# Sliding-window attention into a two-layer MLP: other runs for the query loads, casts and fills at other steps, and a finer token grouping

## The chip, the cores and the metric

The kernel runs on one core of one Trainium2 chip. The metric is the device time of one execution in microseconds, as the median of several runs. The core's engines (TensorE, VectorE, ScalarE, GpSimd, and SyncE, here SP) each work through their own instructions in order and wait for each other on semaphores. Nearly all DMAs are issued from SP's queue.

## The reference

```python
# q, k, v: (8, 8, 576, 64) float32;  w_in (512, 2048), w_out (2048, 512)
scores = matmul(q, k.transpose(0, 1, 3, 2)) / sqrt(64)
mask = abs(pos[:, None] - pos[None, :]) <= 32
attn = softmax(where(mask, scores, -1e9))
x = matmul(attn, v).transpose(0, 2, 1, 3).reshape(8 * 576, 512)
h = x @ w_in
return maximum(0.01 * h, h) @ w_out          # (4608, 512)
```

Each token attends to the 65 tokens around it, eight heads are put side by side to 512 features, and an MLP with a leaky ReLU follows.

## The kernel before

**Two schemes.** Heads are worked in pairs (`NPAIR` = 4 pairs, index `p`). Batches 0 and 1 (`BY_DMA` = 2) are transposed on TensorE. Batches 2 to 7 are loaded as float32 (`load_qk`, L68), cast to bf16 on GpSimd (`cast_qk`, L258, into `qb` and `kb`) and transposed by a DMA (`transpose_dma`, L281): the keys straight into `kz`, the queries into a tile `kT`, from which VectorE copies the two heads to separate places in `qz` (`place_queries`, L293). Values are loaded by `load_v_pairs` (L103, five DMAs for two pairs) into one buffer `vbuf`, and `cast_vw` (L274) casts them into `vw`, where columns of ones beside them give the softmax's sums in the same matmul. The other half of `qz` must be zero (`clear_q`), the padding of `kz` too, and the ones must be set (`ready`, L226); all of this is filled once per buffer set (`sets`, two of them, used by even and odd batches), over space that batches 0 and 1 used before.

**Steps.** One step of the new scheme is one head pair and 256 tokens, taken as four blocks of 64: `score_blocks` (L348) multiplies each block's queries with 128 keys, ScalarE takes the exponential, GpSimd multiplies by `band`, and two steps later `product_blocks` (L364) multiplies by the values and ones, ScalarE moves the sums, and VectorE takes the reciprocal and scales into `xT`. `step` (L558) does step i's product and step i + 2's score, then the queued work: `qk_due` says at which step a pair is cast and transposed, `v_due` when its values are cast. `base(b)` is the first step with tokens of batch b; batch 3's is 24. Right after the cast, `load_qk` and `load_v_pairs` refill the float32 tiles for the next batch. `chore` lets one more fill be issued per call.

**Groups.** The MLP runs over groups of tokens: four of 288 (batches 0 and 1), then two of 256, five of 512 and one of 384. For each group come 16 hidden tiles (`h_tile`: four matmuls, then one eviction by ScalarE with the leaky ReLU, `h_out`), later the output tiles of 128 tokens (`o_tile`: 16 matmuls, one eviction, one store). Hidden and output tiles share four PSUM accumulators (`mmps`).

**Order.** The order is written out by hand up to group 1. From there a small planner adds up the matmul time of hidden and output tiles into a clock and spreads the steps over it (`due`), so that a group's tokens are ready 5 us of that clock before its hidden tiles begin; `spend` runs the steps that are due. SP's queue follows the same program order: loads, transposes and stores are issued one behind the other, each also waiting until the eighth DMA before it has landed.

Of the kernel before, what the change touches and what calls it, by code (L numbers as in the profile page):

```python
# [10 lines left out]
BF16 = mybir.dt.bfloat16  # L11
AF = mybir.ActivationFunctionType
# [4 lines left out]
def kernel(  # L17
# [6 lines left out]
    moe_w_out: bass.AP,  # L24
    out: bass.AP,
):

# [4 lines left out]
    nc = tc.nc  # L32

    B, H, S, D = q.shape
    W = 32
# [4 lines left out]
    NPAIR = H // 2  # L40
    NB = S // 64
# [7 lines left out]
    const = ctx.enter_context(tc.tile_pool(name="const", bufs=1))  # L49
# [13 lines left out]
    qf, kf, vf = {}, {}, {}  # L63
    RUN = S // 96

    BY_DMA = 2

    def load_qk(b, p, behind=None):  # L68

        for into, src, name in ((qf, q, "qf"), (kf, k, "kf")):
            t = fload.tile([96, 2, RUN * D], FP32, name=f"{name}{p}")
            if behind is not None:
                behind.memset(t[0:1, 0, 0:1], 0.0)
                behind = None
            heads = src[b, 2 * p:2 * p + 2]
            if b < BY_DMA:
                nc.sync.dma_start(out=t, in_=heads.rearrange("a (p c) d -> p a (c d)", c=RUN))
            else:  # L80
                nc.sync.dma_start(
                    out=t.rearrange("p a (c d) -> p a c d", d=D),
                    in_=heads.rearrange("a (c p) d -> p a c d", p=96),
                )
            into[b, p] = t
# [17 lines left out]
    def load_v_pairs(b, p):  # L103

        r = slice(2 * p, 2 * p + 4)
        heads = v[b, r]
        for n in range(5):
            rows = slice(W if n == 0 else 0, 128 - W if n == 4 else 128)
            at = 128 * n - W
            nc.sync.dma_start(  # L110
                out=vtile[rows, r, n],
                in_=heads[:, at + rows.start:at + rows.stop].rearrange("a p d -> p a d"),
            )
# [29 lines left out]
    KPAD = S + 2 * W  # L143
    N_Q, N_K, N_V, N_BD = NPAIR * 2 * S, NPAIR * KPAD, NPAIR * NB * 3 * D, NPAIR * NB * 128
    N_SET = N_Q + N_K + N_V
    sets = [const.tile([128, N_SET], BF16, name=f"set{i}") for i in range(2)]
    qT, kbd, vbd, qz, kz, vw = [], [], [], [], [], []
    for t in sets:
        qT.append(t[:, 0:NPAIR * S].rearrange("p (n s) -> p n s", n=NPAIR))
        kbd.append(t[:, N_SET - 2 * N_BD:N_SET - N_BD].rearrange(  # L150
            "p (n m j) -> p n m j", n=NPAIR, j=128))
        vbd.append(t[:, N_SET - N_BD:].rearrange("p (n m j) -> p n m j", n=NPAIR, j=128))
        qz.append(t[:, 0:N_Q].rearrange("p (n a s) -> p n a s", n=NPAIR, a=2))
        kz.append(t[:, N_Q:N_Q + N_K].rearrange("p (n s) -> p n s", n=NPAIR))
        vw.append(t[:, N_Q + N_K:].rearrange("p (n m c d) -> p n m c d", n=NPAIR, c=3, d=D))
# [42 lines left out]
        lo = (16, 0)[hf]  # L198
        nc.gpsimd.tensor_copy(out=mask[hf][:, 1, :, lo:lo + 128], in_=win_f[:, :, 0:128])

    band = const.tile([128, 8, D], BF16)

    def make_band():

        nc.gpsimd.memset(band, 1.0)
        yield
        nc.gpsimd.affine_select(
            out=band, in_=band, compare_op=ALU.is_ge, fill=0.0,
            base=0, channel_multiplier=1, pattern=[[0, 8], [-1, D]],
        )  # L210
        yield
        nc.gpsimd.affine_select(
            out=band, in_=band, compare_op=ALU.is_ge, fill=0.0,
            base=2 * W, channel_multiplier=-1, pattern=[[0, 8], [1, D]],
        )
        yield

    band_parts = make_band()

    def clear_q(i):  # L220
        for p in range(NPAIR):
            for a in range(2):
                nc.vector.memset(qz[i][64 * (1 - a):64 * (1 - a) + 64, p, a], 0.0)
                yield

    def ready(i):  # L226

        nc.vector.memset(kz[i][:, :, 0:W], 0.0)
        nc.vector.memset(kz[i][:, :, KPAD - W:], 0.0)
        yield  # L230
        for p in range(NPAIR):
            nc.vector.memset(vw[i][:, p, :, 1], 1.0)
            yield
        nc.vector.memset(vw[i][0:W, :, 0, 1], 0.0)
        nc.vector.memset(vw[i][128 - W:128, :, NB - 1, 1], 0.0)
        yield

    NPROB = 6
# [12 lines left out]
    OLD = 8 * BY_DMA  # L251
# [22 lines left out]
    def cast_vw(b, p):  # L274

        to, src = vw[b % 2][:, p], vf[b, p].rearrange("p a s d -> p s a d")
        nc.gpsimd.tensor_copy(out=to[:, 0::2, 0:3:2], in_=src)  # L277
        nc.gpsimd.tensor_copy(out=to[0:64, 1::2, 0:3:2], in_=src[64:128, 0:4])  # L278
        nc.gpsimd.tensor_copy(out=to[64:128, 1::2, 0:3:2], in_=src[0:64, 1:5])  # L279

    def transpose_dma(b, p):  # L281
        t = kt.tile([128, S], BF16, name="kT")
        for to, src in ((t, qb), (kz[b % 2][:, p, W:W + S], kb)):
            nc.sync.dma_start_transpose(
                out=to.rearrange("p (c i) -> p c i", c=RUN),
                in_=src[:, p].rearrange("p c a d -> p (c a d)"),
            )
# [60 lines left out]
    def score_blocks(i):  # L348
        p, bs = i % NPAIR, blocks_of(i)
        n = 2 * 64 * len(bs)  # L350
        lo = 512 * (i % 2)
        sc = ps[:, lo:lo + n].rearrange("p (a w i) -> p a w i", a=2, i=64)
        for w, (b, m) in enumerate(bs):
            nc.tensor.matmul(  # L354
                sc[:, :, w], kz[b % 2][:, p, 64 * m:64 * m + 128],
                qz[b % 2][:, p, :, 64 * m:64 * m + 64], start=True, stop=True,
            )
# [3 lines left out]
        nc.gpsimd.tensor_mul(pr, e[:, 0:n], band.rearrange("p w i -> p (w i)")[:, 0:n])  # L361
        probs[i] = pr.rearrange("p (a w i) -> p a w i", a=2, i=64)

    def product_blocks(i):  # L364
# [102 lines left out]
    GROUPS = [(HALF * g, HALF) for g in range(2 * BY_DMA)]  # L467
    t0, new = 0, NTOK - BY_DMA * S
    while t0 < new:
        n = 256 if t0 < 512 else min(512, new - t0)  # L470
        GROUPS.append((t0 % NEW_RING, n))
        t0 += n

# [8 lines left out]
    def h_out(g, f, h):  # L482
        t0, n = GROUPS[g]
        to, h = gT[:, f, t0:t0 + n], h[:, 0:n]
        if g < 2 * BY_DMA:
            to = to.rearrange("p (i c) -> p i c", c=2)
            h = h.rearrange("p (c i) -> p i c", c=2)
        nc.scalar.activation(out=to, in_=h, func=AF.Prelu, alpha=0.01)  # L488

    def h_tile(g, f, n=1):  # L490

        hs = [mmps.tile([128, 512], FP32, name="mm", tag="mm") for _ in range(n)]
        for cs in (range(DMC - 1), (DMC - 1,)) if n > 1 else (range(DMC),):
# [48 lines left out]
    JOINED = 12  # L542
    state = {"done": 0}

    qk_due, v_due = {}, {}
    for b in range(BY_DMA, B):
        for p in range(NPAIR):
            qk_due.setdefault(base(b) + p - (7 if b == BY_DMA else 6), []).append((b, p))
            v_due.setdefault(base(b) + p - 2, []).append((b, p))

    chores = []

    def chore(n=1):
        for _ in range(n):
            while chores and next(chores[0], "end") == "end":
                chores.pop(0)

    def step():  # L558
        i = state["done"]
        if JOINED - 1 <= i < OLD - 1:  # L560
            join(i + 1)
        if i < NC - 2:
            score(i + 2)
        weighted(i)
        place_keys()
        place_queries()
        for b, p in qk_due.get(i, ()):
            cast_qk(b, p)
            transpose_dma(b, p)
            if BY_DMA < b < B - 1:  # L570
                load_qk(b + 1, p)
        if 12 < i <= 12 + NPAIR:
            load_qk(BY_DMA + 1, i - 13)
        if i == 8:
            chores.append(ready(0))
        if OLD - 6 <= i < OLD - 3:
            next(band_parts)
        if i == OLD - 2:
            chores.extend([clear_q(1), ready(1)])
        for b, p in v_due.get(i, ()):  # L580
            cast_vw(b, p)
            if b + 1 < B and p % 2 == 1:
                load_v_pairs(b + 1, p - 1)
        chore(1 if i < OLD - 2 else 2)
        state["done"] += 1

    w_in_r = moe_w_in.rearrange("(c p) f -> p c f", p=128)
# [83 lines left out]
    def second_half():  # L671
# [18 lines left out]
    def second_pair(p):  # L690
        next(second)
# [114 lines left out]
```

## Time and profile before

| | |
|---|---|
| time, median of 3 runs | 329.09 us (328.3 to 329.28) |
| the profiled execution | 327.55 us, span 325.9 us |
| TensorE busy | 299.8 us, 92% of the span |
| VectorE, ScalarE, GpSimd busy | 228.2, 214.1, 198.0 us |
| mean granted TensorE clock | 0.993 |
| moved by DMA | 49.45 MB in 136240 packets |

The span is what the profiler saw of the engines' work; the execution's own time is a little longer. Busy time of TensorE counts pipelined matmuls and so is not the same as full speed. Lines such as "L354" are lines of the kernel before. In lists of waits the columns are total us, number, and the longest; in timelines they are start, duration, engine, line, operation, the tiles written and read, and in brackets the idle time before and what ended it. "PE" is TensorE's matmuls, "DVE" VectorE, "ACT" ScalarE, "POOL" GpSimd, "SPq" SP's DMA queue.

### The profile page before, as it was taken

What the parts mean: (1) busy time and instruction counts of PE and PEld (TensorE: products, weight loads), DVE (VectorE), ACT (ScalarE), POOL (GpSimd) and SP (SyncE); (2) the same over time, 40 slices, a digit from 0 to 9 for tenths busy, and PEclk for the clock granted to TensorE, in tenths of its full rate; (3) what the DMA queues carried; (4) which work ended last, traced back from release to release, by engine and by line L of the source; (5) the groups of instructions that cost most, each with busy time, mean ns of one, the idle gap of its engine ahead of it and who ended that gap; (6) DMA issues with size and microseconds to landing.
All of it is one profiled execution on the core that took longest, in us unless ns stands there. A gap on an engine that the chain in (4) does not pass through costs nothing.

```text
span 325.9 us, 6374 instructions
## 1 busy us (share of the span) xinstructions
PE 299.8 (92%) x2282; PEld 177.1 (54%) x2313; DVE 228.2 (70%) x314; ACT 214.1 (66%) x450; POOL 198.0 (61%) x242
## 2 busy tenths in 40 slices
PE   2679998999997779999999999999999999999995
PEld 1557774574763465854555555555555555444553
DVE  5688777989995769798689867678768766753000
ACT  7596689382873475958954984597469756852731
POOL 8889873987884649677677723667767752110000
PEclk9999999999999799999999999999999999999999
DMA  8999999987998999999899610899673011001001
GB/s 187 228 187 232 268 219 212 226 163 159 201 215 192 196 193 245 173 220 187 195 171 232 169 45 34 164 177 229 135 160 93 1 64 67 0 29 71 32 29 70
DMA packets 136240, 49.45 MB, mean 152 GB/s; under 512 B 124304, under 2 KB 131728, under 8 KB 136208
## 3 DMA queue, kind: packets, MB, share of 16 engines
q1 hardware_dynamic: 131984, 44.84, 70.4%
q0 software_dynamic: 4224, 4.19, 7.9%
q8 instruction: 18, 0.29, 0.4%
q14 instruction: 14, 0.11, 0.1%
HBM read 36.70 MB, written 9.44 MB: 142 GB/s over the span
## 4 chain that ended last, share of the span: by engine, by line
PE 65%; DMA 13%; DVE 8%; POOL 5%; issue 4%; ACT 3%; POOLq 0%; ACTq 0%; DVEq 0%; SPq 0%
PE mm L523 29%; PE mm L477 28%; DMA vbuf<-in_v_dram 5%; DMA kT<-qb 4%; PE ps L354 3%; DVE r L428 3%; DMA qf<-in_q_dram 2%; DVE set L298 2%; PE s L372 2%; PE x L372 2%; DMA set<-kb 1%; POOL qb L264 1%; POOL prob L401 1%; POOL kb L264 1%; ACT e L359 1%
## 5 line engine op out<-in xcount | busy, mean ns | idle before, releaser
L477 PE MATMUL mm<-xT,w_in_bf 128*128 128x512 bf16 (+3 forms) x758 | 134.5, 328 | 0.8 <-ACT gT L488 0.2
L523 PE MATMUL mm<-w_out_bf,gT 128*128 128x512 bf16 (+2 forms) x571 | 128.9, 373 | 1.2
L381 DVE RECIPROCAL r<-r 128x256 f32<-128x256 f32 (+1 forms) x56 | 95.0, 1696 | 36.2 <-ACT r L380 35.6
L361 POOL TENSOR_TENSOR prob<-e,band 128x512 bf16<-128x512 bf16 (+1 forms) x56 | 62.9, 1123 | 77.0 <-ACT e L359 74.0
L488 ACT ACTIVATE gT<-mm 128x512 bf16<-128x512 f32 (+3 forms) x192 | 87.7, 494 | 19.3 <-PE mm L477 15.7
L477 PEld LDWEIGHTS <-w_in_bf 128*128 128x128 bf16 x768 | 73.5, 99 | 46.3 <-issue 0.8
L523 PEld LDWEIGHTS <-gT 128*128 128x128 bf16 x592 | 55.1, 98 | 58.2
L359 ACT ACTIVATE e<-ps 128x512 bf16<-128x512 f32 (+1 forms) x56 | 32.5, 580 | 49.1 <-PE ps L354 41.5
L528 ACT ACTIVATE o_sb<-mm 128x512 f32<-128x512 f32 (+2 forms) x37 | 21.7, 585 | 26.5 <-PE mm L523 21.6
L428 DVE RECIPROCAL r<-s 128x288 f32<-128x288 f32 x16 | 31.2, 1951 | 3.9 <-PE s L423 3.3
L264 POOL CAST kb<-kf 96x768 bf16<-96x768 f32 x32 | 27.8, 870 | 3.9 <-DMA kf<-in_k_dram 3.7
L298 DVE COPY set<-kT 64x576 bf16<-64x576 bf16 x48 | 22.4, 467 | 9.5 <-DMA kT<-qb 8.7
L354 PE MATMUL ps<-set 128*128 128x128 bf16 x216 | 21.9, 219 | 7.0 <-DMA set<-kb 4.5
L354 PEld LDWEIGHTS <-set 128*128 128x128 bf16 x216 | 16.7, 98 | 19.5 <-DMA set<-kb 7.4
L385 DVE TENSOR_TENSOR xT<-s,r 64x256 bf16<-64x256 f32 (+1 forms) x56 | 23.1, 413 | 3.6 <-DVE r L381 0.5
L385 DVE TENSOR_TENSOR xT<-x,r 64x256 bf16<-64x256 f32 (+1 forms) x56 | 23.1, 413 | 3.3
L401 POOL TENSOR_TENSOR prob<-e,mask 128x576 bf16<-128x576 bf16 x16 | 20.3, 1274 | 8.3 <-ACT e L399 7.9
L264 POOL CAST qb<-qf 96x768 bf16<-96x768 f32 x24 | 19.7, 822 | 0.0
L372 PEld LDWEIGHTS <-set 128*128 128x128 bf16 x432 | 18.2, 99 | 1.0 <-issue 0.5
L277 POOL CAST set<-vbuf 128x640 bf16<-128x640 f32 x24 | 17.7, 738 | 0.3 <-DMA vbuf<-in_v_dram 0.3
L278 POOL CAST set<-vbuf 64x512 bf16<-64x512 f32 x24 | 14.6, 610 | 1.5
L279 POOL CAST set<-vbuf 64x512 bf16<-64x512 f32 x24 | 14.6, 608 | 1.2
(70 smaller groups left out, 215.5 us busy)
## 6 DMA issues: line engine op xcount, KB each, us to landing
qf<-in_q_dram SPq DMA_DIRECT2D x32, 288.0 KB, 4.8
kf<-in_k_dram SPq DMA_DIRECT2D x32, 288.0 KB, 5.5
out_dram<-o_sb SPq DMA_DIRECT2D x35, 256.0 KB, 3.5
vbuf<-in_v_dram SPq DMA_DIRECT2D x36, 128.0 KB, 3.7
vbuf<-in_v_dram SPq DMA_DIRECT2D x16, 144.0 KB, 6.2
vbuf<-in_v_dram SPq DMA_DIRECT2D x24, 96.0 KB, 3.4
w_in_bf<-in_moe_w_in_dram POOLq DMA_DIRECT2D x4, 512.0 KB, 8.1
w_out_bf<-in_moe_w_out_dram POOLq DMA_DIRECT2D x4, 512.0 KB, 16.2
```

What stands on the lines that cost most here:

```text
L264: eng.tensor_copy(out=to, in_=tok)
L298: nc.vector.tensor_copy(out=qz[b % 2][r, p, a], in_=t[r])
L354: nc.tensor.matmul(sc[:, :, w], kz[b % 2][:, p, 64 * m:64 * m + 128], qz[b % 2][:, p, :, 64 * m:64 * m + 64], start=True, stop=True,)
L359: nc.scalar.activation(out=e[:, 0:n], in_=ps[:, lo:lo + n], func=AF.Exp, scale=scale)
L361: nc.gpsimd.tensor_mul(pr, e[:, 0:n], band.rearrange("p w i -> p (w i)")[:, 0:n])
L372: nc.tensor.matmul(x[:, a, w], vw[b % 2][:, p, m, a:a + 2].rearrange("p n d -> p (n d)"), pr[:, a, w], start=True, stop=True,)
L381: nc.vector.reciprocal(r[:, 0:n], r[:, 0:n])
L385: nc.vector.tensor_mul(xT[rows, p, t0:t0 + n], x[rows, a], r[rows, 0:n])
L428: nc.vector.reciprocal(r, s)
L477: nc.tensor.matmul(h[:, 0:n], w_in_bf[:, c, ts(f, 128)], xT[:, c, t0:t0 + n], start=(c == 0), stop=(c == DMC - 1),)
L488: nc.scalar.activation(out=to, in_=h, func=AF.Prelu, alpha=0.01)
L523: nc.tensor.matmul(o[:, lo:hi], gT[:, f, t0:t0 + 128], w_out_bf[:, f, lo:hi], start=(f == 0), stop=(f == FFC - 1),)
```

## The change

- From batch 2 on a query load reads two neighbouring tokens in one run of 512 bytes where it read one in 256. The queries of a batch then stand in `qz` in another order (within 192 tokens first the even, then the odd ones). A score's 64 queries are two runs of 32, `band` is built in that order, and `h_out` puts the pairs back in order as it evicts.
- `qk_due` is one step sooner for batches 3 to 7 (`base(b) + p - 7` for all), `v_due` one step sooner for all. The value loads stay at their step (`v_next`), but within a step the order is now casts of q and k, their transposes, casts of values, value loads, then the q and k loads.
- Batch 1's transposed queries move from set 1 to the end of set 0, so that set 1's `qz` can be cleared early.
- The fills are spread anew: clears of `qz` during group 0's hidden tiles, six on ScalarE and six on VectorE, and four on VectorE during group 1's; ones for two pairs on VectorE during group 1's, for the other six on ScalarE at steps 14, 15 and 17 to 20; the pads of `kz` and the edges of the ones on GpSimd. Before they were all on VectorE: the eight clears of set 0's `qz` during group 1's hidden tiles, set 0's pads and ones at steps 8 to 13, and set 1's clears, pads and ones from step 14 on, two per step.
- Four groups of 256 tokens in place of two: 256 four times, 512 four times, 384.

```diff
+            elif into is qf:
+                nc.sync.dma_start(
+                    out=t.rearrange("p a (g e) -> p a g e", g=3),
+                    in_=heads.rearrange("a (g p c) d -> p a g (c d)", g=3, c=2),
+                )
...
-    for t in sets:
-        qT.append(t[:, 0:NPAIR * S].rearrange("p (n s) -> p n s", n=NPAIR))
+    for t, at in zip(sets, (0, N_SET - NPAIR * S)):
+        qT.append(sets[0][:, at:at + NPAIR * S].rearrange("p (n s) -> p n s", n=NPAIR))
...
-    band = const.tile([128, 8, D], BF16)
+    band = const.tile([128, 8, 2, 32], BF16)
...
-    def clear_q(i):
-        for p in range(NPAIR):
+    def clear_q(i, pairs, eng):
+        for p in pairs:
             for a in range(2):
-                nc.vector.memset(qz[i][64 * (1 - a):64 * (1 - a) + 64, p, a], 0.0)
+                r = slice(64 * (1 - a), 64 * (1 - a) + 64)
+                if eng is nc.scalar:
+                    eng.activation(
+                        out=qz[i][r, p, a], in_=zero[r].to_broadcast([64, S]), func=AF.Copy)
+                else:
+                    eng.memset(qz[i][r, p, a], 0.0)
                 yield
-    def ready(i):
-        nc.vector.memset(kz[i][:, :, 0:W], 0.0)
-        nc.vector.memset(kz[i][:, :, KPAD - W:], 0.0)
-        yield
-        for p in range(NPAIR):
-            nc.vector.memset(vw[i][:, p, :, 1], 1.0)
+    def set_ones(i, pairs, eng):
+        for p in pairs:
+            to = vw[i][:, p, :, 1]
+            if eng is nc.scalar:
+                eng.activation(
+                    out=to, in_=one.to_broadcast([128, NB * D]).rearrange("p (m d) -> p m d", d=D),
+                    func=AF.Copy,
+                )
+            else:
+                eng.memset(to, 1.0)
+            nc.gpsimd.memset(vw[i][0:W, p, 0, 1], 0.0)
+            nc.gpsimd.memset(vw[i][128 - W:128, p, NB - 1, 1], 0.0)
             yield
-        nc.vector.memset(vw[i][0:W, :, 0, 1], 0.0)
-        nc.vector.memset(vw[i][128 - W:128, :, NB - 1, 1], 0.0)
+    def clear_k(i):
+        nc.gpsimd.memset(kz[i][:, :, 0:W], 0.0)
+        nc.gpsimd.memset(kz[i][:, :, KPAD - W:], 0.0)
         yield
...
         for w, (b, m) in enumerate(bs):
+            tok = qz[b % 2][:, p].rearrange("p a (g c i) -> p a g c i", c=2, i=96)
+            at = 32 * (m % 3)
             nc.tensor.matmul(
                 sc[:, :, w], kz[b % 2][:, p, 64 * m:64 * m + 128],
-                qz[b % 2][:, p, :, 64 * m:64 * m + 64], start=True, stop=True,
+                tok[:, :, m // 3, :, at:at + 32], start=True, stop=True,
             )
...
-        n = 256 if t0 < 512 else min(512, new - t0)
+        n = 256 if t0 < 1024 else min(512, new - t0)
...
+        else:
+            to = to.rearrange("p (w i c) -> p w i c", i=32, c=2)
+            h = h.rearrange("p (w c i) -> p w i c", c=2, i=32)
...
-            qk_due.setdefault(base(b) + p - (7 if b == BY_DMA else 6), []).append((b, p))
-            v_due.setdefault(base(b) + p - 2, []).append((b, p))
+            qk_due.setdefault(base(b) + p - 7, []).append((b, p))
+            v_due.setdefault(base(b) + p - 3, []).append((b, p))
+            if b + 1 < B and p % 2 == 1:
+                v_next.setdefault(base(b) + p - 2, []).append((b + 1, p - 1))
...
         for b, p in qk_due.get(i, ()):
             cast_qk(b, p)
             transpose_dma(b, p)
+        for b, p in v_due.get(i, ()):
+            cast_vw(b, p)
+        for b, p in v_next.get(i, ()):
+            load_v_pairs(b, p)
+        for b, p in qk_due.get(i, ()):
             if BY_DMA < b < B - 1:
                 load_qk(b + 1, p)
...
-        if i == 8:
-            chores.append(ready(0))
+        if i == OLD - 2:
+            chores.append(set_ones(0, (2, 3), nc.scalar))
+        if i == OLD:
+            chores.extend([clear_k(1), set_ones(1, range(NPAIR), nc.scalar)])
...
-        if i == OLD - 2:
-            chores.extend([clear_q(1), ready(1)])
-        for b, p in v_due.get(i, ()):
-            cast_vw(b, p)
-            if b + 1 < B and p % 2 == 1:
-                load_v_pairs(b + 1, p - 1)
-        chore(1 if i < OLD - 2 else 2)
+        chore()
...
+    chores.extend([clear_q(1, (0, 1), nc.scalar), clear_q(0, (2,), nc.scalar)])
+    more = [clear_q(1, (2, 3), nc.vector), clear_q(0, (3,), nc.vector)]
     for f in range(4, FFC):
         h_tile(0, f)
+        chore()
+        if f % 2 == 1:
+            chore(from_=more)
...
-    chores.append(clear_q(0))
+    chores.extend([clear_q(0, (0, 1), nc.vector), clear_k(0), set_ones(0, (0, 1), nc.vector)])
```

More of the change, by code (lines that the diff above doesn't have):

```diff
@@ L208, in make_band @@
             out=band, in_=band, compare_op=ALU.is_ge, fill=0.0,
-            base=0, channel_multiplier=1, pattern=[[0, 8], [-1, D]],
+            base=0, channel_multiplier=1, pattern=[[0, 8], [-1, 2], [-2, 32]],
         )
@@ L213, in make_band @@
             out=band, in_=band, compare_op=ALU.is_ge, fill=0.0,
-            base=2 * W, channel_multiplier=-1, pattern=[[0, 8], [1, D]],
+            base=2 * W, channel_multiplier=-1, pattern=[[0, 8], [1, 2], [2, 32]],
         )
@@ L218 @@
     band_parts = make_band()
-    def clear_q(i):
-        for p in range(NPAIR):
+    one = const.tile([128, 1], BF16)
+    nc.vector.memset(one, 1.0)
+    def clear_q(i, pairs, eng):
+        for p in pairs:
             for a in range(2):
-                nc.vector.memset(qz[i][64 * (1 - a):64 * (1 - a) + 64, p, a], 0.0)
-                yield
-    def ready(i):
-        nc.vector.memset(kz[i][:, :, 0:W], 0.0)
-        nc.vector.memset(kz[i][:, :, KPAD - W:], 0.0)
-        yield
-        for p in range(NPAIR):
-            nc.vector.memset(vw[i][:, p, :, 1], 1.0)
+                r = slice(64 * (1 - a), 64 * (1 - a) + 64)
[4 more added lines that the diff above has]
+                    eng.memset(qz[i][r, p, a], 0.0)
+                yield
+    def set_ones(i, pairs, eng):
[10 more added lines that the diff above has]
+            nc.gpsimd.memset(vw[i][128 - W:128, p, NB - 1, 1], 0.0)
             yield
-        nc.vector.memset(vw[i][0:W, :, 0, 1], 0.0)
-        nc.vector.memset(vw[i][128 - W:128, :, NB - 1, 1], 0.0)
+    def clear_k(i):
+        nc.gpsimd.memset(kz[i][:, :, 0:W], 0.0)
+        nc.gpsimd.memset(kz[i][:, :, KPAD - W:], 0.0)
         yield
@@ L351, in score_blocks @@
         lo = 512 * (i % 2)
-        sc = ps[:, lo:lo + n].rearrange("p (a w i) -> p a w i", a=2, i=64)
+        sc = ps[:, lo:lo + n].rearrange("p (a w c i) -> p a w c i", a=2, c=2, i=32)
         for w, (b, m) in enumerate(bs):
+            tok = qz[b % 2][:, p].rearrange("p a (g c i) -> p a g c i", c=2, i=96)
+            at = 32 * (m % 3)
             nc.tensor.matmul(
                 sc[:, :, w], kz[b % 2][:, p, 64 * m:64 * m + 128],
-                qz[b % 2][:, p, :, 64 * m:64 * m + 64], start=True, stop=True,
+                tok[:, :, m // 3, :, at:at + 32], start=True, stop=True,
             )
@@ L360, in score_blocks @@
         pr = prob[:, i % NPROB].rearrange("p n c i -> p (n c i)")[:, 0:n]
-        nc.gpsimd.tensor_mul(pr, e[:, 0:n], band.rearrange("p w i -> p (w i)")[:, 0:n])
+        nc.gpsimd.tensor_mul(pr, e[:, 0:n], band.rearrange("p w c i -> p (w c i)")[:, 0:n])
         probs[i] = pr.rearrange("p (a w i) -> p a w i", a=2, i=64)
@@ L543, with chore @@
     state = {"done": 0}
-    qk_due, v_due = {}, {}
+    qk_due, v_due, v_next = {}, {}, {}
     for b in range(BY_DMA, B):
         for p in range(NPAIR):
-            qk_due.setdefault(base(b) + p - (7 if b == BY_DMA else 6), []).append((b, p))
-            v_due.setdefault(base(b) + p - 2, []).append((b, p))
+            qk_due.setdefault(base(b) + p - 7, []).append((b, p))
+            v_due.setdefault(base(b) + p - 3, []).append((b, p))
+            if b + 1 < B and p % 2 == 1:
+                v_next.setdefault(base(b) + p - 2, []).append((b + 1, p - 1))
     chores = []
[L553 to L556, printed above, removed]
+    def chore(from_=chores):
+        while from_ and next(from_[0], "end") == "end":
+            from_.pop(0)
     def step():
```

## The prediction

> **What bounds the kernel now.** I read the page's slices first, then the waits of TensorE, then the timelines of TensorE and of SP in the stretch where TensorE waits.
>
> ```profile
> PE   2679998999997779999999999999999999999995
> PEclk9999999999999799999999999999999999999999
> DMA  8999999987998999999899610899673011001001
> DMA packets 136240, 49.45 MB, mean 152 GB/s; under 512 B 124304, under 2 KB 131728, under 8 KB 136208
> ```
>
> One slice is 8.15 us. TensorE is full except at the start, in slices 13 to 15 (98 to 122 us) and at the end; from 150 us on it is busy 31.79 of 32 us and more, so nothing can be won there. The DMA engines are full up to about 180 us, nearly all with packets under 512 bytes. In slices 14 and 15 the granted clock falls too. TensorE's waits from 80 to 160 us:
>
> ```profile
> PE ps L354 <- DMA set<-kb: 4.5, 2, 2.4
> PE ps L354 <- DVE set L298: 2.5, 2, 2.1
> ```
>
> Columns: total us, times, longest. Both are the scores of batch 3's first blocks: they wait for the keys that the DMA transposes, or for VectorE's copy of the queries that it transposes. TensorE's timeline has the three large ones (2.38, 2.13, 2.07 us, sum 6.58), the fourth (0.39 us) stands at 149.70:
>
> ```profile
> 104.32 0.34 PE L354 MATMUL ps<-set 128*128 128x128 bf16 x3 [2.38 <-DMA set<-kb]
> 109.67 0.37 PE L354 MATMUL ps<-set 128*128 128x128 bf16 x3 [2.13 <-DVE set L298]
> 110.28 4.22 PE L477 MATMUL mm<-xT,w_in_bf 128*128 128x256 bf16 x24
> 120.27 0.34 PE L354 MATMUL ps<-set 128*128 128x128 bf16 x3 [2.07 <-DMA set<-kb]
> ```
>
> The third line is their second price: 24 matmuls take 4.05 us in the chain, 0.169 each, where 15 of the same shape at 130 us take 1.62 (0.108). The windows give a granted clock of 0.57, 0.50 and 0.59 for 109.7 to 110.5, 112 and 113.5 us: 0.8·0.43 + 1.5·0.50 + 1.5·0.41 = 1.7 us lost. Why the transposes are late is in SP's timeline:
>
> ```profile
> 93.97 1.37 SPq L81 DMA_DIRECT2D kf<-in_k_dram  x1
> 95.44 2.19 SPq L529 DMA_DIRECT2D out_dram<-o_sb  x1
> 97.73 2.60 SPq L110 DMA_DIRECT2D vbuf<-in_v_dram  x5
> 100.44 1.20 SPq L284 DMA_TRANSPOSE kT<-qb  x1
> 101.75 1.20 SPq L284 DMA_TRANSPOSE set<-kb  x1
> ```
>
> The cast of pair 0 (GpSimd, 90.07 and 90.84) was done at 91.7; SP came to its transposes 8.8 us later, through a queue that it issues in order. SP, fed by full DMA engines, sets the time here.
>
> **The change, part by part.** *Queries in 512-byte runs.* A query load of batch 2 on has 576 packets, not 1152. Under load the 256-byte loads hold SP 1.3 to 1.4 us (54.15 to 59.7), unloaded 0.57; 1536-byte loads unloaded 0.40 (L79's median). Bounds for one query load: nothing saved (the bytes stay), or half of 1.33, 0.66; more time is excluded by L79's rows. I take 0.4, for packets are what fills these engines. Eight such loads (batches 2 and 3) stand ahead of batch 3's first transposes: 3.2 us (0 to 5.3). The Trainium skill, DMA: Bandwidth & Descriptors, Specifications, puts the least transfer for line rate at 512 bytes; by it and the 435 GB/s that it gives for all engines a 295 kB load would take an estimated 0.7 us, and a forecast by it alone would drop the 1.0 us of waits left over below: 322.0.
>
> *Casts and transposes one step sooner.* Batch 3's pair 0 goes from step 18 to 17, and on SP from behind the five value loads to ahead of them: 97.73 in place of 100.44, 2.7 us. With the 3.2 its issue is at 94.5, still behind the cast. Then SP issues the two transposes (2.5), the five value loads that now follow (2.7), batch 4's q and k (1.2): pair 1 at 100.9. The pitch from pair to pair is 104.32 − 100.44 = 3.9: pair 2 at 104.8, pair 3, with one output store (1.3), at 110.0. Keys land 1.3 + 2.7 us after that (the key transposes' median time to landing; once 4.5): 98.5, 104.9, 108.8, 114.0. Due: without waits, before's first score of batch 3 stood at 101.7. The planner's clock puts it 1.8 us later (45.3 for 43.5), since a 256-token group is wanted where a 512 was and fewer steps are wanted in that time; costs below add 1.1. That gives 104.6 and, at 3.06 + 0.45 us per step, 108.1, 111.6, 115.1. All four are in time, the last by 1.1 us; a landing of 4.5 would make it 0.7 late, and VectorE's in-order query copies wait sooner. I leave 1.0 us of the 6.58 (0 to 2.5) and count the 1.7 of clock as won, since the single gap of 1.04 us at 50 us leaves the clock at 1.00 in its window. The 0.39 at 149.7 goes as well: batch 4's transposes leave a step sooner, with SP not behind.
>
> *Fills off VectorE.* From 50 to 82 us TensorE waits 0.6 + 0.4 + 0.2 = 1.2 us for VectorE's scaling or reciprocals. VectorE is full there; five fills or pairs of fills of 0.34 to 0.69 us between 63.5 and 83 leave it, 2.8 us. The 1.2 goes (at worst it stays).
>
> *Fills put on ScalarE.* Six of 64x576 come into group 0's hidden-layer tiles, from 28 us: 0.66 to 0.68 us each by the copies of that width (L314, L270), 4.0 us, against ScalarE's idle 0.18 + 0.56 + 0.71 + 1.50 = 2.95 up to 36.9. Four accumulators hide about four tiles of 0.49; tile 11 is then the first to find its buffer unread. VectorE gets six of 0.298 in the same chain, whose idle is 0.48, so the last scaling is about 1.3 late for group 1: the same 1.3, overlapping. I take 1.3 (0 to 2.0). Four fills of ones fall in steps 17 to 20. From 84.3 to 93.2 ScalarE is already busy 8.56 of 8.90 us; two of 0.66 lie between its evictions there, and each can hold TensorE by up to 0.7 beyond the buffers: 1.0 (0 to 2.0). The other two ones meet ScalarE's idle (0.84 and 1.60 us near 73 and 76) and cost nothing; without it they would cost 0.7 each. A rule against this part: the Trainium skill, ScalarE: Activation LUTs, Rules for kernel authors, puts cheap elementwise work on VectorE, up to about three times faster. By 3 · 0.298 the six fills would be an estimated 5.4 us and the sum 1.4 worse; no fill of this width on ScalarE is in the trace, but L314 and L270 are nearer.
>
> *256 for 512.* One 512-token group becomes two of 256: 64 matmuls and weight loads more. 2 · 0.1081 − 0.2156 = 0.6 ns each pair: 0.04 us, say 0.1. Evictions: 16 · (2 · 0.389 − 0.596) = 2.9 us more ScalarE, in stages of which before's (130.0 to 138.6) has ScalarE busy 8.31 of 8.60 and TensorE waiting 0.17 for L488: 0.4 for two such stages (0 to 2.0).
>
> *At nothing.* The eviction that puts pairs back in order: before's 288-wide one, ordered so, takes 419 ns, the line between 256 (389) and 384 (490) gives 414. Score operands in runs of 32: same 128 columns. The band's new order: same three instructions. Key pads and edges on GpSimd: a dozen fills of 0.3 or less, in its idle (0.3 to 1.6 us per step). The second batch's queries in set 0: written from 39.8, last reader (L439) done at 35.2.
>
> Sum: −6.58 − 1.70 − 0.39 − 1.20 = −9.87; +1.0 + 1.3 + 1.0 + 0.4 + 0.1 = +3.8; net −6.1. The profiled execution took 327.55 (span 325.9), so 321.5; the median of the runs, 329.09, is 1.54 above it: 323.0.
>
> **Rivals.** *Only the order helps.* If 512-byte packets take twice as long as 256-byte ones, transposes start at 97.7; keys land at 101.7, 108.1, 112.0, 117.2 (or 119): waits of 0.4 and 2.1 to 3.9, and the clock may fall again. −9.87 + 3.0 + 1.7 + 2.8 = −2.4: 326.7. For it: bytes are unchanged; against: 0.40 against 0.57 unloaded.
>
> *Costs at their upper ends.* 2.0 + 2.0 + 2.0 + 0.1 + 2.5 = 8.6, and the clock stays low for 1.7: +0.4, 329.5, no change. For it: ScalarE is nearly full in three of the stages.
>
> *Slower: GpSimd blocked by the value loads.* Value casts move a step up too. Step 15's cast of batch 2's pair 2 waits for loads that landed at 83.6 in before (its cast, a step later, idled 0.32 for them). GpSimd, in order, holds the mask products of steps 18 and 19 and then batch 3's casts behind it. With loads at 83.6 the product for step 18 ends at 87.0, TensorE wants it at 87.9: it decides from a landing of about 84.5. Then TensorE waits some 2 us there, batch 3's casts pass 94, and the old waits and the low clock come back: −1.2 + 2.8 + 2.0 = +3.6, 332.7. Against: SP issues those loads after batch 2's quicker query loads.
>
> *Not as said.* The loads shorten SP's queue only if SP waits for DMA; if the store at 95.44 waited for its data instead, packets are no matter and the first rival's time results.
>
> **How the numbers follow.** Forecast 0.68 (319.5 to 325.5), first and last rival together 0.14, upper ends 0.06, slower 0.12. A run tells about 0.3% (1.0 us) from no change. Faster 0.68 + 0.14 = 0.82, same 0.06, slower 0.12. Range: 319.8, nearly all costs at 0 (−9.87 gives 319.2), to 327.9, which takes in the first rival.
>
> **What would show it.** Right: no wait of over 1 us for batch 3's scores, a clock of 1.00 from 98 to 126 us, SP's transposes of pair 0 by 95 us; query loads below 1 us on SP under load; TensorE waiting for ScalarE's evictions near 34 and 87 us by about 1 us each. Wrong: the score waits still there, GpSimd idle behind vbuf at 80 to 85 us, or more than 2 us of waits for L488's successor in the 256-token stages.

## The result, and the profile after

The changed kernel took 325.0 us (median of four runs, 323.49 to 326.01) where the kernel before took 329.18: a ratio of 0.987, interval 0.9822 to 0.9919. A second set of runs, experiment 9 below, gave 323.6 us and 0.9871 [0.9841, 0.9901]. It is faster, by about 4.2 us (1.3%); the forecast was 323.0 us. The profiled execution took 323.49 us (span 321.8), 4.06 less than that of before.

The same rows of the page, after:

```profile
PE   2778898999999989999999999999999999999995
PEclk9999999999999999999999999999999999999999
DMA  8999999977999999999989903995492011001001
DMA packets 122416, 49.45 MB, mean 154 GB/s; under 512 B 96656, under 2 KB 117904, under 8 KB 122384
```

One slice of the dent of slices 13 to 15 is left (slice 15, 112.6 to 120.7 us, at 83%), the dip in the clock's row is gone, and a shallower dent has come into slices 4 to 6 (84, 85 and 95% busy, where before had 91, 98 and 99%). The bytes are the same; 13,824 packets are gone, which is 24 query loads of 576.

TensorE's timeline after, batch 3's first scores (start, duration, in brackets the idle time before and what ended it). There are two waits where there were three, 1.97 us where there were 6.58:

```profile
108.66 0.33 PE L377 MATMUL ps<-set 128*128 128x128 bf16 x3 [0.64 <-DVE set L319]
117.64 0.33 PE L377 MATMUL ps<-set 128*128 128x128 bf16 x3 [1.33 <-DVE set L319]
```

SP's queue after, the stretch that was shown of before:

```profile
90.72 1.06 SPq L87 DMA_DIRECT2D kf<-in_k_dram  x1
91.87 1.07 SPq L555 DMA_DIRECT2D out_dram<-o_sb  x1
93.05 1.71 SPq L305 DMA_TRANSPOSE kT<-qb  x1
...
96.12 3.86 SPq L116 DMA_DIRECT2D vbuf<-in_v_dram  x5
...
101.20 2.02 SPq L305 DMA_TRANSPOSE kT<-qb  x1
```

Pair 0's transposes are issued at 93.05 in place of 100.44, ahead of the five value loads; pairs 1 to 3 follow at 101.20, 105.81 and 111.14.

The price is in TensorE's timeline in group 0's hidden tiles, where no wait stood before:

```profile
32.38 0.65 PE L500 MATMUL mm<-xT,w_in_bf 128*128 128x288 bf16 x4 [0.45 <-ACT gT L514]
33.38 0.65 PE L500 MATMUL mm<-xT,w_in_bf 128*128 128x288 bf16 x4 [0.35 <-ACT gT L514]
34.52 0.65 PE L500 MATMUL mm<-xT,w_in_bf 128*128 128x288 bf16 x4 [0.49 <-ACT gT L514]
```

ScalarE's fills (0.68 us each) stand between the evictions there:

```profile
31.92 0.41 ACT L514 ACTIVATE gT<-mm 128x288 bf16<-128x288 f32 x1
32.36 0.68 ACT L233 ACTIVATE set<-zero 64x576 bf16<-64x576 bf16 x1
32.94 0.39 ACT L514 ACTIVATE gT<-mm 128x288 bf16<-128x288 f32 x1
```

Group 3 has two waits of 0.37 us of the same kind, at 88.47 and 92.89.

What still holds the two scores is in VectorE's timeline after:

```profile
102.63 1.68 DVE L319 COPY set<-kT 64x576 bf16<-64x576 bf16 x2
104.35 1.75 DVE L404 RECIPROCAL r<-r 128x256 f32<-128x256 f32 x1
106.20 0.86 DVE L408 TENSOR_TENSOR xT<-s,r 64x256 bf16<-64x256 f32 x2
107.09 1.51 DVE L319 COPY set<-kT 64x576 bf16<-64x576 bf16 x2
...
116.97 0.62 DVE L319 COPY set<-kT 64x576 bf16<-64x576 bf16 x2 [1.75 <-DMA kT<-qb]
```

From 99.9 to 108.6 VectorE is busy without a gap, so pair 1's copies come behind a step's reciprocal and scaling; its queries had landed at 106.1, its keys at 106.6. Pair 3's copies wait for the transpose itself: issued at 111.14, landed at 116.94, 5.80 us later. Its keys are no sooner. They were issued at 112.57 and landed 5.0 us later, at 117.6, just as the copies ended, and TensorE's weight load (PEld) waited for them:

```profile
117.61 0.19 PEld L377 LDWEIGHTS <-set 128*128 128x128 bf16 x3 [1.62 <-DMA set<-kb]
```

### The profile page after: what moved, and what is told of

It is laid out like the page before. It is cut to its first block, busy times and chain, and to the rows that moved or that the text cites. A ratio compares the mean times of both kernels' runs of the same rounds, so it can differ in the third digit from the quotient of the medians.

```text
span 321.8 us, 6551 instructions
## 1 busy us (share of the span) xinstructions
PE 300.6 (93%) x2377; PEld 182.0 (57%) x2377; DVE 226.5 (70%) x295; ACT 221.8 (69%) x478; POOL 199.5 (62%) x262
## 4 chain that ended last, share of the span: by engine, by line
PE 79%; ACT 8%; DVE 7%; issue 2%; DMA 2%; POOL 1%; ACTq 0%; POOLq 0%; DVEq 0%
PE mm L549 35%; PE mm L500 32%; PE ps L377 4%; ACT gT L514 2%; PE s L395 2%; DMA kT<-qb 2%; PE x L395 2%; DVE set L319 2%; DVE r L451 1%; PE ps L417 1%; DVE r L404 1%; PE x L462 1%; ACT e L422 1%; DVE set L356 1%; POOL prob L424 1%
## 5 line engine op out<-in xcount | busy, mean ns | idle before, releaser
L500 PE MATMUL mm<-xT,w_in_bf 128*128 128x288 bf16 (+3 forms) x832 | 135.6, 313 | 2.5 <-ACT gT L514 2.4
L549 PE MATMUL mm<-w_out_bf,gT 128*128 128x512 bf16 (+2 forms) x592 | 131.8, 373 | 0.0
L500 PEld LDWEIGHTS <-w_in_bf 128*128 128x128 bf16 x832 | 79.0, 98 | 44.8 <-issue 4.2
L514 ACT ACTIVATE gT<-mm 128x288 bf16<-128x288 f32 (+3 forms) x208 | 87.9, 469 | 15.0 <-PE mm L500 11.8
L285 POOL CAST kb<-kf 96x768 bf16<-96x768 f32 x32 | 27.1, 847 | 5.0 <-DMA kf<-in_k_dram 4.8
L319 DVE COPY set<-kT 64x576 bf16<-64x576 bf16 x48 | 25.3, 527 | 2.7 <-DMA kT<-qb 1.7
L377 PEld LDWEIGHTS <-set 128*128 128x128 bf16 x216 | 16.9, 98 | 13.5 <-DMA set<-kb 1.6
```

The source lines that it names most:

```text
L285: eng.tensor_copy(out=to, in_=tok)
L319: nc.vector.tensor_copy(out=qz[b % 2][r, p, a], in_=t[r])
L377: nc.tensor.matmul(sc[:, :, w], kz[b % 2][:, p, 64 * m:64 * m + 128], tok[:, :, m // 3, :, at:at + 32], start=True, stop=True,)
L500: nc.tensor.matmul(h[:, 0:n], w_in_bf[:, c, ts(f, 128)], xT[:, c, t0:t0 + n], start=(c == 0), stop=(c == DMC - 1),)
L549: nc.tensor.matmul(o[:, lo:hi], gT[:, f, t0:t0 + 128], w_out_bf[:, f, lo:hi], start=(f == 0), stop=(f == FFC - 1),)
```

## The experiments

Theory: SP's queue set the time. Shorter query loads and the new order bring batch 3's transposes in ahead of need; the fills on ScalarE give a part back. Rivals: the order alone does it; the groups do it, by wanting the steps later; the fills decide. The kernel before ran beside each set: 328.4 us in experiments 1 to 4, 328.51 in 5 to 8, 328.21 in 9 to 12.

**1. The change without its runs of 512 bytes.**

```diff
-            elif into is qf:
-                nc.sync.dma_start( ... two neighbouring tokens in one run ... )
-                tok[:, :, m // 3, :, at:at + 32], start=True, stop=True,
+                qz[b % 2][:, p, :, 64 * m:64 * m + 64], start=True, stop=True,
```

> The changed kernel with the query loads back in 256-byte runs (and the query order, band and eviction order that go with them); all else as changed. If packets are what fills the DMA engines (as forecast), SP comes to batch 3's first transposes near 96 to 97 us instead of 93.05, all four pairs are some 3 us later, and TensorE's waits for batch 3's scores grow from 2.0 us to 4 to 6, perhaps with the half clock again: 327 to 330 us. If the packets do not matter and only the order and the step do (the first rival): as the changed kernel, 324 to 326.

Measured: 328.11 us, ratio 0.9992 [0.9973, 1.0012]. The whole gain is gone. TensorE's timeline has 4.70 us of waits for batch 3's scores back (and 1.06 us for batch 4's keys, at 151.37), and the window from 98 to 126 us has a granted clock of 0.94, as before:

```profile
110.50 0.33 PE L370 MATMUL ps<-set 128*128 128x128 bf16 x3 [3.20 <-DVE set L314]
...
120.97 0.33 PE L370 MATMUL ps<-set 128*128 128x128 bf16 x3 [1.50 <-DVE set L314]
```

Its SP queue and its GpSimd timeline say why the sooner step alone is not enough:

```profile
98.39 1.23 SPq L300 DMA_TRANSPOSE kT<-qb  x1
```

```profile
84.92 0.72 POOL L293 CAST set<-vbuf 128x640 bf16<-128x640 f32 x1 [3.33 <-DMA vbuf<-in_v_dram]
```

Transposes start 5.34 us later than with 512-byte runs (93.05). And the value cast, a step sooner now, finds its loads not landed and holds GpSimd 3.33 us; with the runs it waits 0.70. This is the first half of the prediction's slower rival, seen. Its second half did not come: TensorE shows no wait for a masked product there.

**2. The change with the steps and the order of before.**

```diff
-            qk_due.setdefault(base(b) + p - 7, []).append((b, p))
-            v_due.setdefault(base(b) + p - 3, []).append((b, p))
+            qk_due.setdefault(base(b) + p - (7 if b == BY_DMA else 6), []).append((b, p))
+            v_due.setdefault(base(b) + p - 2, []).append((b, p))
...
```

> The changed kernel with casts, transposes and value casts at the steps and in the order of the kernel before; all else as changed. If the step is worth the 2.7 us on SP that were forecast, SP comes to batch 3's first transposes near 96 us, and the waits for its scores grow by 1 to 3 us: 326 to 328 us. If the queue had room to spare after the shorter loads: as the changed kernel, 324 to 326.

Measured: 324.79 us, 0.9909 [0.9877, 0.9942]. Its profiled execution was the longest of the six, 327.35 us. In it pair 0's transposes are at 99.30, the waits 1.23, 1.06 and 2.62 us, more than in the change, and the granted clock is 0.50 from 122 to 124 us. The mean granted clock was 0.995 in this execution and 0.999 or 1.00 in the other five, so the median, within 1.2 us of the change's, is not the time of what this profile shows.

**3. The change with two groups of 256 tokens.**

```diff
-        n = 256 if t0 < 1024 else min(512, new - t0)
+        n = 256 if t0 < 512 else min(512, new - t0)
```

> The changed kernel with two groups of 256 tokens and five of 512, as before; all else as changed. If the finer groups only put off when batch 3's scores are wanted (by 1.8 to 2.3 us of the planner's clock), the waits for them grow by 1.5 to 2.5 us: 326 to 328 us. If the groups matter by ScalarE's evictions alone: 0.3 us faster, not to be told from the changed kernel.

Measured: 325.56 us, 0.9918 [0.9891, 0.9945]. Transposes at 93.94, waits 1.33, 1.15 and 1.53: 2.0 us more than in the change, as the first expectation had it, in an execution of 326.39 us, the longest of six. The median is 0.6 to 2.0 us above the change's.

**4. The change with the fills of before** (all on VectorE, at their old steps, batch 1's queries in set 1 again).

```diff
-            chores.append(set_ones(0, (2, 3), nc.scalar))
-        if i == OLD:
-            chores.extend([clear_k(1), set_ones(1, range(NPAIR), nc.scalar)])
+            chores.extend([clear_q(1), ready(1)])
...
-    chores.extend([clear_q(1, (0, 1), nc.scalar), clear_q(0, (2,), nc.scalar)])
-    more = [clear_q(1, (2, 3), nc.vector), clear_q(0, (3,), nc.vector)]
```

> The changed kernel with all fills on VectorE at the steps of the kernel before (and batch 1's queries back in set 1); all else as changed. By the traces the new fills cost TensorE 1.8 us behind ScalarE in group 0, 0.4 near 48 us and 1.1 in group 3, and gave 1.9 back between 60 and 84 us. If these add up to the end: 0 to 1.5 us faster than the changed kernel, 323.5 to 325. If TensorE's early lateness is only taken out of its waits for batch 3 (the transposes are then late by SP and VectorE's queue, whatever TensorE did before): the waits near 107 to 118 us are larger or smaller by just that, and the time is the same. If VectorE's load was what mattered: 2 us slower or more.

Measured: 323.21 us (322.81 to 323.43), 0.9852 [0.983, 0.9874]. The waits of groups 0 and 3 for ScalarE are gone, VectorE's of 0.60, 0.28 and 0.44 us near 80 are back.

**5 to 7. The kernel before with the 512-byte runs alone; with runs and groups; with runs and the sooner step.** The edits are those of the diff, one part at a time.

> The kernel before with the 512-byte query runs alone (and the query order, band and eviction order that go with them). If the runs carry the gain by themselves, SP comes to batch 3's first transposes 5 us sooner than in the kernel before (near 95 us), and two of the three waits and the half clock go: 323.5 to 325.5 us. If runs help only together with the sooner step and the finer groups: 326 to 328 us.

> The kernel before with the 512-byte runs and the four groups of 256. If the finer groups are worth the 1.8 to 2.3 us by which they put off batch 3's scores, it is 1 to 2 us faster than with the runs alone, 322.5 to 324 us; if the groups do nothing, equal to the runs alone.

> The kernel before with the 512-byte runs and the sooner step (with its order in a step), in the old groups. If the step is worth the 2.7 us of SP's queue that were forecast, 1 to 2 us faster than with the runs alone, 322.5 to 324 us. If VectorE's own queue of copies and reciprocals holds batch 3's scores by then, equal to the runs alone.

| the kernel before with | us | ratio | waits of batch 3's scores | pair 0's transposes on SP |
|---|---|---|---|---|
| runs | 325.22 | 0.9912 [0.9891, 0.9932] | 0.86, 2.33, 1.18, 1.81 | 99.69 |
| runs, groups | 323.18 | 0.9863 [0.9832, 0.9893] | 1.23, 0.74, 1.15 | 97.65 |
| runs, step | 323.53 | 0.9876 [0.9853, 0.9899] | 1.65, 0.51 | 93.86 |
| runs, step, groups (experiment 4) | 323.21 | 0.9852 [0.983, 0.9874] | 1.63, 1.05 | 92.16 |

The runs are worth 3.3 us by themselves. Step or groups on top is worth 1.7 to 2.0 us, both together no more than one. But the way in which the runs alone were expected to work did not show. They hardly move SP: 99.69 where before had 100.44. The waits add up to 6.18 us, where before had 6.58:

```profile
109.11 0.33 PE L362 MATMUL ps<-set 128*128 128x128 bf16 x3 [2.33 <-DVE set L304]
```

The two profiled executions (326.0 and 327.55 us) differ by 0.4 us in these waits and 0.4 in batch 4's, by the 1.7 us of low clock (1.00 in place of 0.94 from 98 to 126 us), and by 0.8 the other way in waits before 98 us. So what the runs alone win there is mostly the clock. The mean granted clock was 0.998 or more in all six of their executions and 0.995 or less in seven of the eleven of the kernel before beside them. The other half of the 3.3 us no kept profile shows. With the sooner step on top the score waits fall to 2.16 us. In SP's queue of the kernel with the runs alone the five value loads, still ahead of the transposes, take 4.59 us where they took 2.60:

```profile
94.99 4.59 SPq L116 DMA_DIRECT2D vbuf<-in_v_dram  x5
99.69 1.20 SPq L290 DMA_TRANSPOSE kT<-qb  x1
```

SP was there 2.7 us sooner (94.99 against 97.73), and the loads absorbed 2.0 of it. GpSimd does not explain that: SP's value loads wait 1.5 us for it from 86 to 101 us, and waited 2.3 in before. What lengthened them stays open.

**8. The change with its fills moved to steps where their engines had idle time.**

```diff
+        if i == 8:
+            chores.extend([clear_k(0), set_ones(0, (0, 1), nc.scalar), clear_q(1, (0, 1), nc.scalar)])
...
+            chores.extend([clear_k(1), clear_q(1, (2, 3), nc.vector), set_ones(1, range(NPAIR), nc.vector)])
...
+    chores.append(clear_q(0, range(NPAIR), nc.vector))
```

Group 0's hidden tiles have no fills; from step 16 on two are issued per step.

> The changed kernel with its fills where the engines are idle in its trace: none in group 0; eight clears on VectorE in group 1; ones of set 0 and three clears of set 1 on ScalarE at steps 9 to 15; the rest of set 1's clears and ones on VectorE from step 16 on, two a step. If the fills cost what TensorE's timeline shows (1.8 in group 0, 1.1 in group 3, 0.4 near 48 us) and VectorE's relief near 60 to 84 us is kept: 1 to 2 us faster than with the old fills (323.2), 321 to 322.5 us. If TensorE's early time is taken back by its waits for batch 3: as with the old fills, 323 us, with longer waits near 107 to 118 us.

Measured: 324.6 us, 0.9896 [0.9857, 0.9934]. From 24 to 50 us TensorE is busy 24.72 us where the change has 23.00, as wanted; but it is waited for later:

```profile
108.72 0.33 PE L377 MATMUL ps<-set 128*128 128x128 bf16 x3 [2.89 <-DVE set L319]
...
113.28 0.33 PE L377 MATMUL ps<-set 128*128 128x128 bf16 x3 [0.76 <-DVE set L319]
...
119.77 0.33 PE L377 MATMUL ps<-set 128*128 128x128 bf16 x3 [2.71 <-DVE set L319]
```

6.36 us in place of 1.97, with the first transposes at 94.78: TensorE comes earlier (pair 1's first block at 105.61, not 107.80) to a queue that comes 1.7 us later. The time fits neither expectation; the longer waits are those of the second.

**9. The change again.**

> The changed kernel unaltered, beside the kernel before, for more runs of it: so far 325.0 us (323.49 to 326.01, four runs, ratio 0.987), while the same with the fills as before had 323.21 (ratio 0.9852 [0.983, 0.9874]). If the new places of the fills cost about 1.8 us, as the TensorE waits at 31 to 35 us and in group 3 (2.4 us in the list of waits) say, the ratio is 0.988 to 0.991 (324.6 to 325.5 us). If the distance between the two was the scatter of few runs, it is 0.985 or 0.986 (323.3 to 323.9 us).

Measured: 323.6 us (322.65 to 324.52, six runs), 0.9871 [0.9841, 0.9901]: the time as if it had been scatter, the ratio between the two expectations. Its waits from 26 us on are like those of the first profile: 2.4 us in 7 for ScalarE in the hidden tiles (2.4 in 7 there), 2.9 in 3 for batch 3's scores (2.0 in 2). So 0.4 to 1.8 us separate it from experiment 4, and these runs alone do not settle it.

**10. As experiment 4, and for batch 3 one of two query copies on ScalarE.**

```diff
-                nc.vector.tensor_copy(out=qz[b % 2][r, p, a], in_=t[r])
+                if b == 3 and a == 1:
+                    nc.scalar.activation(out=qz[b % 2][r, p, a], in_=t[r], func=AF.Copy)
+                else:
+                    nc.vector.tensor_copy(out=qz[b % 2][r, p, a], in_=t[r])
```

> The change with the fills of before (323.21 us), and for batch 3 alone one of the two copies of each pair's queries on ScalarE (four copies of 64x576) instead of VectorE. There the scores waited 1.63 us for pair 1, whose two copies ended at 108.04 behind a reciprocal of 1.75 us and scalings of 0.86 us on VectorE, and 1.05 us for pair 3, whose copies began when the transposes landed at 115.87. If VectorE's queue holds pair 1 and the landing pair 3: one copy less is 0.4 to 0.6 us, so pair 1 waits about 1.1 us, pair 3 about 0.7 (its copies run side by side), together 1.8 in place of 2.7: 322.4 us (ratio 0.982 to 0.984). If transposes landing hold both, nothing moves: 323.2 us. If the copies on ScalarE, 0.68 us each by the fills of that shape, hold its exponentials and evictions back, the waits move there and it is 323.2 to 324.5 us.

Measured: 328.19 us, 1.0008 [0.9983, 1.0033]: four copies of 0.68 us cost 5 us. The score waits did fall, to 0.3 us. But ScalarE works in order too. Its timeline, then TensorE's:

```profile
105.70 0.68 ACT L305 ACTIVATE set<-kT 64x576 bf16<-64x576 bf16 x1 [2.76 <-DMA kT<-qb]
106.41 0.60 ACT L542 ACTIVATE o_sb<-mm 128x512 f32<-128x512 f32 x1
...
110.01 0.68 ACT L305 ACTIVATE set<-kT 64x576 bf16<-64x576 bf16 x1 [1.72 <-DMA kT<-qb]
110.71 0.60 ACT L542 ACTIVATE o_sb<-mm 128x512 f32<-128x512 f32 x1
```

```profile
111.36 0.60 PE L488 MATMUL mm<-xT,w_in_bf 128*128 128x256 bf16 x4 [3.58 <-ACT o_sb L542]
```

ScalarE stands still until the transpose lands, with an eviction behind the copy; the buffers fill up and TensorE waits 3.58 us, and the clock falls to 0.94 in that window. No theory had priced the wait in front of the copy, only the copy.

**11. As experiment 4, with the value loads of pairs 2 and 3 behind pair 3's transposes.**

```diff
-                v_next.setdefault(base(b) + p - 2, []).append((b + 1, p - 1))
+                at = base(b) + p - 2 if p == 1 else base(b + 1) - 4
+                v_next.setdefault(at, []).append((b + 1, p - 1))
```

> The change with the fills of before (323.21 us), and the second value load of each batch (pairs 2 and 3, five DMAs, 3.89 us on SP at 95.25, between the transposes of pair 0 and pair 1) moved behind the transposes of pair 3. Casts of pair 3 were done at 100.2 us, while SP came to its transposes at 110.25, so SP's queue sets when they start. If it does: transposes of pairs 1 to 3 about 3.9 us sooner (96.4, 101.0, 106.4), pair 3's land by 112 and its score does not wait (1.05 us gone), pair 1's wait for VectorE stays at 1.0 to 1.6 us: 322.2 us (ratio 0.981 to 0.983). If the landings under load give the time back (the loads behind them move as well), pair 3 starts sooner but lands at the same time: 323.2 us. If the values come too late for their casts three steps on, GpSimd holds the masked products there and it is 324 us or more.

Measured: 326.86 us, 0.9956 [0.9926, 0.9986]. Pair 3's transposes came at 107.83 (110.25 in experiment 4) and its score did not wait, as the theory said; pair 1 waited 1.31 us, for VectorE. But the third expectation came as well. GpSimd's and TensorE's timelines:

```profile
116.58 0.72 POOL L283 CAST set<-vbuf 128x640 bf16<-128x640 f32 x1 [4.88 <-DMA vbuf<-in_v_dram]
...
148.64 0.72 POOL L283 CAST set<-vbuf 128x640 bf16<-128x640 f32 x1 [7.24 <-DMA vbuf<-in_v_dram]
```

```profile
151.96 0.39 PE L380 MATMUL x<-prob,set 128*128 128x64 bf16 x8 [1.99 <-POOL prob L369]
```

GpSimd waits for values that are now late, the masked products stand behind the cast, and TensorE waits for them. This is the slower rival's mechanism with both its halves, though only from 152 us on and without its low clock.

**12. Experiments 10 and 11 together.**

> Both edits: one copy of each of batch 3's pairs on ScalarE, and the second value load behind pair 3's transposes. If VectorE's queue holds pair 1 and SP's queue pair 3, both gains add: waits for batch 3's scores 1.1 us or less in place of 2.7, 321.4 to 322.0 us (ratio 0.979 to 0.981), the fastest of all. If one cause holds both pairs, it is as the better of the two alone, 322.2 to 322.5 us. If what is won is waited for elsewhere (as where the fills were moved to idle engines, 324.6 us in place of 321 to 322.5), 323.2 us.

Measured: 326.07 us, 0.9951 [0.9924, 0.9977]. Waits of 0.91 and 4.21 us for ScalarE's eviction, 1.5 for GpSimd's masked products, 0.8 for the scores. Both faults are there, and no expectation's time came.

Experiments 4 and 6 (323.2 us) are the fastest of all kernels run. Their intervals overlap with that of the change, so that they beat it is likely, not shown.

## Why the prediction was right

The likeliest case came true: faster, because batch 3's transposes come nearly in time. By its steps:

- **What bounds it.** Confirmed in the main. With pair 0's transposes on SP at 98.4 to 100.4 us the score waits are 4.7 to 6.6 us (the kernel before, experiments 1, 2 and 5), at 92.2 to 94.2 they are 2.0 to 4.0 (the change, experiments 3, 4, 7 and 9). Experiment 6 (97.65, 3.1) and experiment 8 (94.78, 6.4) show the other side: the waits also depend on when TensorE comes. Of the clock, the prediction read a fall in slices 14 and 15; the row has it in slice 14 alone (0.79).
- **Query runs, 3.2 us of SP (0 to 5.3).** Mis-sized, and not a sum. Taken back from the change, they are 5.34 us of SP (98.39 against 93.05), the upper bound; added to the kernel before, 0.75. All else in the change without them is 2.05 us (100.44 to 98.39; 2.7 was predicted for the order alone), both together 7.39 (5.9 predicted). The prediction added two terms that depend on each other; that their sum came near is in part luck. Nor is the saving spread over eight loads: in the busy stretches query loads still hold SP 1.1 to 1.5 us, not below 1, and batch 2's loads of queries and keys take 9.6 us of SP in both kernels. It shows in the next stretch, from batch 3's first query load to pair 0's transposes (in before, to the value loads ahead of them). With the same loads and stores in it, that stretch takes 13.7 us (79.39 to 93.05) in place of 16.9 (80.81 to 97.73).
- **Issue and landing.** 94.5, 100.9, 104.8 and 110.0 were forecast, 93.05, 101.20, 105.81 and 111.14 came. The scores began at 104.73, 107.80, 112.24 and 116.10 where 104.6, 108.1, 111.6 and 115.1 were due. The order of time was right to 1.5 us.
- **1.0 us of waits left (0 to 2.5).** 2.0 in one profile, 2.9 in the other, outside the bound; the sign "no wait of over 1 us" failed by pair 3's 1.33. The step that failed is the landing. Keys were to land at 98.5, 104.9, 108.8 and 114.0; they landed at 99.5, 106.6, 111.0 and 117.6. For pair 3 that is 1.1 us of issue and 2.3 of landing (5.0 us where 2.7 was taken). From 79 to 118 us key transposes had a median of 4.0 us to landing in place of 3.3 in before, query transposes 5.3 in place of 4.5; that the loads issued among them do this is likely, not shown. VectorE's queue, which holds pair 1, was named, not priced.
- **The clock's 1.7 us and the 0.39 us.** Right in both profiles: 1.00 from 98 to 126 us, no wait at batch 4. It does not hold for each execution: one of the first four (326.01 us) had a mean granted clock of 0.993, as the profiled one of before.
- **VectorE's 1.2 us.** Its waits are gone.
- **Fills on ScalarE, 1.3 in group 0.** 1.29 us by the three waits, 1.74 by when the last product of the group starts (36.50 in place of 34.76), and 0.44 us more at 48.34, where a score waits for VectorE. Group 3: 1.0 forecast, 0.74 by its two waits, about 0.9 by its matmuls' times.
- **The fills' net, +1.1 us.** Three pairs of kernels differ in them alone: 323.21 and 323.6 to 325.0 (experiments 4, 9), 323.18 and 324.79 (6, 2), 323.53 and 325.56 (7, 3). New places cost 0.4 to 2.0 us. Each pair alone is at the limit of what the intervals tell apart; all three point one way. Experiment 8 suggests that the waits of group 0 can't simply be added to the time: without most of them TensorE waited longer for the transposes, which came later there.
- **256-token stages, 0.4.** Two waits of 0.17 us, at 127.08 and 160.08: 0.34.
- **Rivals.** "Only the order helps" is refuted by experiment 1: order, step, groups and new fills without the runs gain nothing together (328.11 us, where the rival had 326.7). The order by itself, without the new fills, was not run; what the fills cost, 0.4 to 2.0 us, is the most that this can hide. "Costs at their upper ends" did not come. The slower rival's mechanism is real, but decided by the landing: the cast that it named starts at 82.05 in the change, inside its limit of 84.5, at 84.92 in experiment 1.

By the terms as measured in the profile the sum is −4.6 − 1.7 − 0.4 − 1.2 + 1.7 (group 0, with the 0.44) + 0.7 + 0.3 = −5.2 against −4.06 of the profiled execution; −6.1 was forecast. Of the 1.1 us between the first two about 0.6 is what groups 0 and 3 lost beyond their listed waits (0.45 and 0.2, above); 0.5 is not placed.

What was not forecast is that step and groups replace each other. By its timelines, less all waits from 26 us on, TensorE comes to batch 3's scores 1.1 to 1.9 us later with the finer groups (and SP comes to pair 0's transposes 0.9 to 2.0 us sooner), while the step has these transposes 5.5 to 6.3 us sooner; both close the same gap, and what stays after either (pair 1 on VectorE's queue, pair 3 on its landing) neither moves.

## What to carry to other kernels

Two edits that close the same gap don't add: after the first, ask what holds the remainder. An instruction that waits for a DMA costs its engine the wait, not its own length, and all that is queued behind it: put it on the engine whose queue nobody is waiting for. Work moved sooner needs its inputs sooner, and a fix at the front of a kernel was worth nothing here where a later queue didn't start sooner with it.

## What was not expected of the hardware

- **VectorE's copies beside GpSimd's work.** Copies of 64x576 bf16 take 0.30 us alone, 0.67 to 0.94 us while GpSimd casts or multiplies; the chain of the change has 0.94 and 0.73 for pair 0, 0.84 and 0.67 for pair 1, 0.30 and 0.32 for pair 3, just after GpSimd's cast had ended at 116.83. The Trainium skill, SBUF — State Buffer, section "SBUF: two separate sides", describes one pair of ports that one of the two, VectorE in a mode that uses it or GpSimd, holds for a whole instruction while the other waits; by that rule a copy waits for the GpSimd instruction that runs, and these rows agree. The four slow copies each end 0.16 or 0.17 us after a GpSimd instruction does (103.41, 104.15, 107.77 and 108.44 us).
- **The clock falls after short gaps, but not always.** In before it was 0.50 to 0.59 from 109.7 to 113.5 us, right behind the wait of 2.13 us and 5 us after that of 2.38. In experiment 2 it was 0.50 after a wait of 2.62 us; in experiment 8 waits of 2.89 and 2.71 us left it at 1.00. The Trainium skill, TensorE: Matmul & The Clock Gate, Part 1, gives about 3.4 us without work as what lowers it; the longest gap of before after 26 us was 2.38, so the measurement decides, and length alone does not tell which gap costs the clock. Executions of one kernel differ too: in the 29 of the kernel before beside experiments 9 to 12 the mean granted clock was 0.988 to 1.00.
- **An in-order eviction queue amplifies.** One ScalarE copy that waited 1.72 us for its transpose, on top of one that had waited 2.76, became 3.58 us of TensorE and a lower clock.
